# Two token mixers in one kernel: a new written order of all its pieces, and first loads in halves over three queues

## The chip, the cores and the metric

The kernel runs on one NeuronCore of one Trainium2 chip. The metric is the device time of one execution in microseconds (us). Three executions of the kernel before took 786.13, 786.30 and 788.06 us; the median is 786.3.

## What is computed

The reference chains two blocks. The first is a recurrent attention over 768 steps for 4 batches and 8 heads with a state of 40 by 40; the second is a feed-forward block on 3072 tokens of width 320 with a hidden width of 2048 and the activation h cos(h).

```python
for t in range(S):                                  # S = 768
    y[:, :, t] = einsum('bhd,bhde->bhe', r_t, state)
    Sa = einsum('bhde,bhe->bhd', state, a_t)
    state = state * w_t - outer(Sa, b_t) + outer(v_t, k_t)
x = y.transpose(0, 2, 1, 3).reshape(3072, 320)
h = x @ w_in                                        # 320 x 2048
out = (h * cos(h)) @ w_out                          # 2048 x 320
```

The arrays r, k, v, w, a, b are float32; w_in and w_out arrive as 8-byte numbers and are turned into float32 on the chip.

## The kernel before

**Tiling.** The 768 steps are cut into 24 chunks of 32 (C = 32). A chunk has 4 batches times 32 steps = 128 partitions. Within a chunk the recurrence is written as small matrix products with one triangular inverse per chunk; four chunks share one inversion. From chunk to chunk only the state is handed on. Two chunks make one group of the feed-forward block (line 95): 256 tokens, 12 groups. A group walks over the hidden width in 4 parts (j = 0 to 3).

**The order is written out by hand.** All instructions of the kernel are issued by one string, PLAN (lines 17 to 93), of some 1200 tokens. Each token calls one small function (table ACTS, line 954), which emits instructions on several engines. Every engine executes its own instructions strictly in the order in which the tokens stand, so the string fixes five queues at once: TensorE (PE), VectorE (DVE), ScalarE (ACT), GpSimd (POOL) and SyncE (SP, which issues DMAs). A wait at the head of one queue holds everything behind it on that engine.

**Tokens of the attention, for chunk c.** `L` and `ld` load one of r, k, v, w, a, b (line 229): four DMAs, one for each batch, of 40 KB each. `L:c:name:queue:part` of the start names the queue (s = SP, a = ACT, p = POOL) and the part: l = batches 0 and 1, r = batches 2 and 3, x = all four. The tiles of r, k and v exist once (line 216), so the load of the next chunk waits until POOL has read the last one. `pw`, `pa`, `pb`, `pn` (lines 425 to 524) transpose w, a, b of two chunks, scan the decay, form reciprocals (line 452) and the coupling matrix. `sf`, `sc`, `ss` (lines 242 to 263) fetch w of four later chunks, scan it on DVE (nine instructions) and store it. `is`, `ip`, `it`, `ih`, `F`, `S` (lines 531 to 618) invert the triangular matrix of four chunks: `is` transposes, the 15 steps `ip` are DVE alone, `it` and `ih` transpose on DVE, and `F` and `S` complete the off-diagonal halves with 64 tiny matmuls each. `in` and `kn` (lines 620 to 629) are POOL: they copy v and r to padded tiles and multiply k. `v`, `k`, `g` transpose v, r, k and form their products on PE (lines 631 to 686). `t`, `q`, `x`, `s`, `z` (lines 689 to 818) are the chain from chunk to chunk; `z` ends in eight DVE instructions (lines 803 and 810) and five POOL instructions (804 and 815). `tk` stores the chunk's result to DRAM and `tb` loads it back transposed as tokens xT, both by SP (lines 820 to 840).

**Tokens of the weights.** Twenty pieces of w_in and w_out: `wf` fetches (SP), `wt` takes exponent and mantissa apart (two DVE instructions, one ACT), `wm` makes the mantissa (one DVE, one ACT), `wg` sets the sign and `wp` multiplies (one DVE each); lines 300 to 341.

**Tokens of the feed-forward block, for group g and part j.** `fa` and `fb` are the first product (lines 843 to 897) with the phase instructions on ACT and DVE behind them, `y` is the rest of the cosine and the product (lines 887 to 900), `sd` the second product (line 902), `o` the store (line 917). `fa:0:0` can start when tokens of chunks 0 and 1 are back.

**Filling.** `B`, `K` and `P` (lines 924 to 951) emit matmuls on a zero tile, whose results nobody uses.

```python
"L": first_load, "ld": lambda c, n: load(c, n),
...
for token in PLAN.split():
    do(token)
```

Of the kernel before, what the change touches and what calls it, by code (L numbers as in the profile page):

```python
# [38 lines left out]
ss:3 kn:6 ld:7:k r:10 pb:8 fa:1:2 q:5 fb:1:2 pn:8 in:6 sd:1:1:0 y:1:2:1 y:1:2:0 x:5 y:1:2:2 sd:1:1:1 fa:1:3  # L39
ld:7:r s:5 sp:8 ld:7:v S:4:2:1 fb:1:3 y:1:3:0 y:1:3:1 z:5 sd:1:2:1 S:4:3:1 tk:5 t:6 r:11 v:6 k:6 pw:10 pa:10  # L40
ld:12:b g:6 tb:5 ld:12:w y:1:3:2 o:0:1 pb:10 kn:7 sd:1:2:0 pn:10 k:7 in:7 v:7 r:12 fa:2:0 is:8 ij:8:31 ij:8:30
q:6 fb:2:0 y:2:0:1 x:6 sd:1:3:1 y:2:0:0 y:2:0:2 ld:13:a ij:8:29 ij:8:28 ld:8:v ij:8:27 ij:8:26 ld:8:r sd:1:3:0
ij:8:25 ld:12:a s:6 o:1:0 in:8 sd:2:0:0 fa:2:1 ij:8:24 fb:2:1 z:6 ld:8:k kn:8 y:2:1:1 y:2:1:0 sd:2:0:1 y:2:1:2
g:7 fa:2:2 ld:13:w v:8 k:8 pw:12 t:7 ld:9:v ij:8:23 ij:8:22 ij:8:21 ij:8:20 ij:8:19 pa:12 q:7 tk:6 fb:2:2 x:7
ij:8:18 ij:8:17 ij:8:16 ld:13:b sd:2:1:0 tb:6 ld:14:a s:7 y:2:2:0 y:2:2:1 ld:9:k r:13 y:2:2:2 sd:2:1:1 ld:9:r
in:9 z:7 ij:8:15 ij:8:14 fa:2:3 fb:2:3 y:2:3:1 g:8 o:1:1 ld:14:w ij:8:13 ij:8:12 sd:2:2:0 y:2:3:0 sf:4
sd:2:2:1 kn:9 ij:8:11 ij:8:10 k:9 v:9 ij:8:9 y:2:3:2 t:8 tk:7 ij:8:8 g:9 ij:8:7 ij:8:6 sd:2:3:1 ij:8:5 ij:8:4
tb:7 fa:3:0 ij:8:3 ij:8:2 ld:14:b q:8 ld:10:v ld:10:r fb:3:0 ld:15:w in:10 y:3:0:0 ld:15:b ij:8:1 x:8 pb:12
sd:2:3:0 ie:8 y:3:0:2 ld:10:k y:3:0:1 sc:4 s:8 fa:3:1 fb:3:1 y:3:1:1 z:8 ld:15:a o:2:0 sd:3:0:0 tk:8 y:3:1:0
ld:11:r y:3:1:2 sd:3:0:1 sd:3:1:0 pn:12 r:15 sp:12 t:9 fa:3:2 o:2:1 q:9 fb:3:2 x:9 y:3:2:1 sd:3:1:1 y:3:2:0  # L50
y:3:2:2 kn:10 ld:11:k s:9 k:10 pw:14 v:10 fa:3:3 r:14 tb:8 z:9 fb:3:3 y:3:3:0 ld:11:v ld:16:b g:10 sd:3:2:1
y:3:3:1 pb:14 tk:9 t:10 pa:14 kn:11 k:11 in:11 y:3:3:2 ss:4 tb:9 pn:14 sd:3:2:0 ld:16:w r:16 fa:4:0 q:10
fb:4:0 x:10 is:12 ij:12:31 v:11 sd:3:3:1 ij:12:30 ij:12:29 ij:12:28 y:4:0:1 ld:12:v ij:12:27 y:4:0:0 ij:12:26
ij:12:25 ld:16:a ld:12:r y:4:0:2 sd:3:3:0 o:3:0 ij:12:24 ij:12:23 in:12 fa:4:1 sd:4:0:0 ld:17:w s:10 fb:4:1
y:4:1:1 y:4:1:0 ld:12:k z:10 y:4:1:2 tk:10 ld:17:a sd:4:0:1 g:11 t:11 fa:4:2 ij:12:22 ij:12:21 tb:10 ij:12:20
sd:4:1:0 ij:12:19 ij:12:18 ij:12:17 q:11 fb:4:2 x:11 kn:12 k:12 ld:17:b pw:16 ij:12:16 ij:12:15 v:12 ij:12:14
pa:16 ld:18:a s:11 sd:4:1:1 r:17 y:4:2:1 ld:13:v y:4:2:0 y:4:2:2 o:3:1 ld:18:w ij:12:13 z:11 ld:13:k fa:4:3
fb:4:3 ij:12:12 ij:12:11 tk:11 y:4:3:0 g:12 ld:13:r in:13 sd:4:2:0 sd:4:2:1 y:4:3:1 ij:12:10 kn:13 sf:5 v:13
k:13 y:4:3:2 ij:12:9 t:12 ij:12:8 g:13 ij:12:7 ij:12:6 ij:12:5 ij:12:4 ij:12:3 ij:12:2 sd:4:3:0 tb:11 ld:19:b
ij:12:1 ld:14:k ie:12 fa:5:0 ld:18:b q:12 ld:14:r fb:5:0 y:5:0:1 y:5:0:0 x:12 sd:4:3:1 y:5:0:2 sd:5:0:1 sc:5  # L60
ld:19:w fa:5:1 s:12 ld:14:v in:14 fb:5:1 y:5:1:0 z:12 tk:12 o:4:0 sd:5:0:0 pb:16 y:5:1:1 sp:16 t:13 pn:16
o:4:1 ss:5 kn:14 k:14 v:14 pw:18 y:5:1:2 fa:5:2 ld:19:a r:18 r:19 q:13 fb:5:2 y:5:2:1 x:13 sd:5:1:1 s:13
y:5:2:0 y:5:2:2 ld:15:r sd:5:1:0 z:13 ld:20:w tb:12 sd:5:2:0 fa:5:3 g:14 ld:15:k ld:15:v kn:15 ld:20:b fb:5:3
y:5:3:1 sd:5:2:1 pb:18 tk:13 t:14 pa:18 tb:13 y:5:3:0 y:5:3:2 in:15 k:15 r:20 fa:6:0 q:14 fb:6:0 pn:18 y:6:0:1
v:15 is:16 ij:16:31 ij:16:30 ij:16:29 ij:16:28 ld:16:v ij:16:27 ld:21:w sd:5:3:0 y:6:0:0 y:6:0:2 x:14 ij:16:26
ij:16:25 ld:20:a ld:16:r o:5:0 in:16 ij:16:24 sd:5:3:1 ld:17:r fa:6:1 ij:16:23 ld:21:b s:14 fb:6:1 ld:21:a
y:6:1:1 y:6:1:0 z:14 r:21 tk:14 sd:6:0:0 v:16 t:15 ij:16:22 ij:16:21 ij:16:20 g:15 sd:6:0:1 y:6:1:2 fa:6:2
tb:14 q:15 ij:16:19 ij:16:18 ij:16:17 fb:6:2 sd:6:1:0 y:6:2:0 x:15 ld:16:k kn:16 ld:17:k ij:16:16 pw:20 pa:20
k:16 ld:22:a s:15 sd:6:1:1 y:6:2:2 y:6:2:1 z:15 ij:16:15 ij:16:14 ld:22:w ij:16:13 o:5:1 fa:6:3 fb:6:3 y:6:3:1
ld:17:v in:17 g:16 ij:16:12 ij:16:11 ij:16:10 kn:17 sd:6:2:1 sd:6:2:0 y:6:3:0 tk:15 tb:15 y:6:3:2 fa:7:0  # L70
ij:16:9 ij:16:8 t:16 v:17 k:17 ld:22:b q:16 ld:23:w ij:16:7 ld:18:r fb:7:0 g:17 ij:16:6 y:7:0:0 y:7:0:2
ld:18:k sd:6:3:0 y:7:0:1 ld:18:v ij:16:5 in:18 ij:16:4 pb:20 x:16 sd:6:3:1 ij:16:3 ij:16:2 ld:23:b ij:16:1
fa:7:1 ie:16 s:16 sd:7:0:0 ld:23:a fb:7:1 z:16 kn:18 y:7:1:0 o:6:0 y:7:1:1 r:23 o:6:1 sd:7:0:1 tk:16 pn:20
y:7:1:2 r:22 fa:7:2 t:17 sp:20 pw:22 v:18 tb:16 k:18 pa:22 q:17 fb:7:2 y:7:2:1 x:17 sd:7:1:0 ld:19:r s:17
sd:7:1:1 ld:19:k y:7:2:0 y:7:2:2 z:17 ld:19:v kn:19 sd:7:2:1 fa:7:3 fb:7:3 g:18 sd:7:2:0 tk:17 t:18 y:7:3:1
y:7:3:0 y:7:3:2 pb:22 tb:17 k:19 fa:8:0 fb:8:0 y:8:0:1 q:18 y:8:0:0 pn:22 sd:7:3:0 is:20 in:19 ld:20:r
ij:20:31 y:8:0:2 sd:7:3:1 ij:20:30 ij:20:29 x:18 ij:20:28 ld:20:v ij:20:27 ij:20:26 v:19 fa:8:1 s:18 fb:8:1
# [924 lines left out]
```

## Time and profile before

| what | us |
|---|---|
| median of the runs | 786.3 |
| the profiled execution | 787.34 |
| its span, first to last instruction | 785.6 |
| PE busy | 743.9 (95%) |
| DVE busy | 488.4 (62%) |
| ACT busy | 386.2 (49%) |
| POOL busy | 173.4 (22%) |

The profiled execution has 1.7 us outside its span, and is 1.0 us above the median of the runs.

The profile is that of one execution. A row of the timeline gives the start from the span's start, the time, the engine, the line of the kernel, the operation, what it writes and reads, and in square brackets how long the engine sat idle before it and what ended that. "issue" means that nothing in the profile explains the wait. Sums below are made against this execution's own time and then set against the median.

### The profile page before, as it was taken

What the parts mean: (1) busy time and instruction counts of PE and PEld (TensorE: products, weight loads), DVE (VectorE), ACT (ScalarE), POOL (GpSimd) and SP (SyncE); (2) the same over time, 40 slices, a digit from 0 to 9 for tenths busy, and PEclk for the clock granted to TensorE, in tenths of its full rate; (3) what the DMA queues carried; (4) which work ended last, traced back from release to release, by engine and by line L of the source; (5) the groups of instructions that cost most, each with busy time, mean ns of one, the idle gap of its engine ahead of it and who ended that gap; (6) DMA issues with size and microseconds to landing.
All of it is one profiled execution on the core that took longest, in us unless ns stands there. A gap on an engine that the chain in (4) does not pass through costs nothing.

```text
span 785.6 us, 39628 instructions
## 1 busy us (share of the span) xinstructions
PE 743.9 (95%) x17828; PEld 574.8 (73%) x17828; DVE 488.4 (62%) x1095; ACT 386.2 (49%) x772; POOL 173.4 (22%) x334
## 2 busy tenths in 40 slices
PE   5767899998999999999999999999999999999997
...
DVE  7979789884555787545876447776536684333331
...
PEclk9959999998999999999999999999999999999999
...
GB/s 96 157 179 158 146 147 116 107 90 47 103 67 68 50 104 53 55 86 39 46 118 34 99 75 39 50 79 43 48 46 10 58 46 36 37 15 39 19 18 17
DMA packets 183304, 55.79 MB, mean 71 GB/s; under 512 B 157152, under 2 KB 178656, under 8 KB 183136
## 3 DMA queue, kind: packets, MB, share of 16 engines
...
q8 instruction: 140, 2.29, 1.2%
q0 software_dynamic: 256, 0.33, 0.2%
...
q14 instruction: 28, 0.23, 0.1%
...
## 4 chain that ended last, share of the span: by engine, by line
PE 86%; DMA 3%; issue 3%; SPq 2%; POOL 2%; DVE 2%; ACT 1%; ACTq 0%; POOLq 0%; DVEq 0%
PE ph L184 28%; PE po L184 27%; PE x0ps L184 5%; PE dps L184 5%; PE gram L184 4%; PE sps L184 3%; PE vT L408 2%; PE qps L184 2%; SPq L235 2%; PE sT L694 2%; PE below L184 1%; PE wT L408 1%; PE busy L184 1%; PE nps L184 1%; PE kT L408 1%
## 5 line engine op out<-in xcount | busy, mean ns | idle before, releaser
L184 PE MATMUL po<-w_out_sb,gT 128*128 128x320 f32 x768 | 225.6, 440 | 2.8 <-issue 1.5
L184 PE MATMUL ph<-xT,w_in_sb 128*128 128x256 f32 x768 | 185.9, 388 | 1.0 <-issue 0.5
L184 PEld LDWEIGHTS po<-w_out_sb,gT 128*128 128x128 f32 x768 | 140.6, 190 | 59.4 <-issue 5.9
L184 PEld LDWEIGHTS ph<-xT,w_in_sb 128*128 128x128 f32 x768 | 142.1, 191 | 33.6 <-issue 12.4
L884 DVE SCALAR_TENSOR_TENSOR turns<-turns,ph 128x512 f32<-128x512 f32 x96 | 64.2, 684 | 128.2 <-ACT turns L882 128.0
L882 ACT ACTIVATE turns<-ph,rnd 128x512 f32<-128x512 f32 x96 | 64.1, 687 | 118.3 <-PE ph L184 115.3
L804 POOL TENSOR_TENSOR qz<-qz,wc 128x160 f32<-128x160 f32 x92 | 40.5, 465 | 253.6 <-DVE qz L803 253.6
L892 DVE TENSOR_TENSOR gT<-ph,turns 128x512 f32<-128x512 f32 x96 | 65.1, 685 | 40.9 <-ACT turns L889 40.9
L889 ACT ACTIVATE turns<-turns,half_pi 128x512 f32<-128x512 f32 x96 | 69.5, 724 | 3.1
L888 ACT ACTIVATE turns<-turns 128x512 f32<-128x512 f32 x96 | 60.0, 625 | 6.9 <-DVE turns L884 6.8
L184 PE MATMUL ph<-xT,w_in_tail 64*64 64x256 f32 (+1 forms) x528 | 54.2, 392 | 0.0
L712 ACT COPY qz<-qps 40x256 f32<-40x256 f32 x92 | 33.8, 367 | 37.1 <-PE qps L184 35.4
L546 DVE TENSOR_TENSOR inv<-inv,inv_tmp 128x31 f32<-128x31 f32 (+15 forms) x124 | 47.5, 383 | 4.3
L452 DVE RECIPROCAL rw<-nat_w 128x320 f32<-128x320 f32 x20 | 42.8, 2142 | 7.3 <-DMA nat_w<-wd 7.3
L542 DVE TENSOR_TENSOR inv_tmp<-u,inv 128x31 f32<-128x31 f32 (+15 forms) x124 | 44.7, 361 | 3.1
L803 DVE TENSOR_TENSOR qz<-dps,qz 128x160 f32<-128x160 f32 x92 | 29.1, 316 | 17.6 <-PE dps L184 17.4
L756 ACT COPY sm<-sps 128x160 f32<-128x160 f32 x48 | 13.9, 293 | 52.1 <-PE sps L184 42.8
L184 PEld LDWEIGHTS ph<-xT,w_in_tail 64*64 64x64 f32 (+1 forms) x528 | 31.9, 157 | 9.3 <-issue 5.3
L815 POOL TENSOR_TENSOR yt<-yt,wb 128x512 f32<-128x512 f32 x24 | 32.0, 1332 | 23.0 <-DVE yt L810 23.0
L453 POOL TENSOR_TENSOR bn<-nat_b,rw 128x320 f32<-128x320 f32 x22 | 19.3, 879 | 73.7 <-DVE rw L452 26.9
...
L673 ACT COPY vvm<-gram 128x128 f32<-128x128 f32 x48 | 12.2, 264 | 39.0 <-PE gram L184 29.4
...
## 6 DMA issues: line engine op xcount, KB each, us to landing
...
```

The costliest lines, as they stand in the source:

```text
L184: nc.tensor.matmul(o, lhsT=lhsT, rhs=rhs, start=start, stop=stop, skip_group_check=True)
L452: nc.vector.reciprocal(rw, wn)
L542: nc.vector.tensor_tensor(tmp, u[:, j : j + 1, :j].to_broadcast([P, C - j, j]), x[:, j:, j : j + 1].to_broadcast([P, C - j, j]), ALU.mult,)
L546: nc.vector.tensor_tensor(x[:, j:, :j], x[:, j:, :j], tmp, ALU.subtract)
L712: nc.scalar.copy(pick(qz[rows], f * (NZ - C), (NZ, 2 * B), (1, C)), ps[f][rows, : 2 * B * C].rearrange("p (i t) -> p i t", t=C),)
L804: nc.gpsimd.tensor_tensor(z, z, wc.rearrange("p (f m b) -> p f m b", f=2, m=2)[:, :, :, bb] .unsqueeze(3).to_broadcast([P, 2, 2, D]), ALU. ...
L815: nc.gpsimd.tensor_tensor(yt.rearrange("p j b t -> p (j b) t"), yt.rearrange("p j b t -> p (j b) t"), wx, ALU.mult)
L882: nc.scalar.activation(t, u, ACTF.Identity, bias=rnd, scale=1.0)
L884: nc.vector.scalar_tensor_tensor(t, t, -ROUND, u, ALU.add, ALU.subtract)
L888: nc.scalar.activation(t, t, ACTF.Abs)
L889: nc.scalar.activation(t, t, ACTF.Sin, bias=half_pi, scale=-2.0 * math.pi)
L892: nc.vector.tensor_tensor(gT[:, 2 * e : 2 * e + 2, :n], phs[e], ns[e].rearrange("p (f t) -> p f t", f=2), ALU.mult)
```

## The change

Only the string PLAN changes. The same pieces are issued, with the same number of filling matmuls (78 in `B`, 98 in `K`, 60 in `P`) and the same 20 weight pieces, in another order from the first token to the last. Two things are different besides the order. The loads of chunks 0 to 3 (six names, four chunks, four batches: 96 DMAs) are all written in halves of two batches: 48 half loads stand where there were 10 whole loads of a, b and w, 4 halves of w, and 11 `ld` tokens for r, k and v. And 38 of these 96 DMAs are on POOL's queue instead of 8; 4 stay on ACT's, 54 are on SP's. From chunk 4 on, all loads are on SP as before.

The diff, cut to the start, the first inversion of chunks 4 to 7, and the end:

```diff
-L:2:w:s:x L:1:w:a:r L:1:a:s:x B:4 L:0:w:a:r L:0:w:s:l L:1:w:s:l L:3:w:s:x L:0:a:s:x L:0:b:p:x L:3:b:s:x
-L:2:b:s:x L:1:b:p:x pw:0 pa:0 pw:2 pb:0 L:3:a:s:x B:4 L:2:a:s:x pa:2 pn:0 B:4 pb:2 lo:0 sf:1 sc:1 pn:2 lo:2
-ld:0:vr in:0 v:0 sp:0 wf:1 wt:1 ld:0:k B:3 is:0 ip:0:15 ip:0:14 ip:0:13 ip:0:12 B:5 ip:0:11 ip:0:10 kn:0
-ld:1:r wf:0 k:0 ip:0:9 g:0 ip:0:8 ip:0:7 ip:0:6 ip:0:5 ip:0:4 ip:0:3 ld:1:k ld:1:v kn:1 ip:0:2 ip:0:1 it:0
-ih:0 B:4 ss:1 k:1 in:1 v:1 g:1 x:0 ld:2:k F:0:0:0 wm:1 wf:2 wt:2 wm:2 S:0:0:0 wf:3 wg:2 wg:1 ld:2:r wp:1 s:0
-B:3 wp:2 wt:0 wf:4 wf:7 ld:2:v wt:3 wm:0 z:0 sf:2 B:5 t:1 wm:3 F:0:1:0 wg:3 B:6 wf:6 wg:0 wp:0 wp:3 B:3 q:1
-wt:7 wt:4 wm:4 wm:7 wg:4 wp:4 in:2 ld:3:r wg:7 wf:8 kn:2 ld:3:k x:1 wp:7 wf:5 K:6 wf:10 B:5 wf:9 k:2 S:0:1:0
-K:14 wt:6 wm:6 v:2 wt:8 wm:8 wg:6 wp:6 wg:8 g:2 K:4 tk:0 wt:5 wm:5 ld:3:v wg:5 wp:5 wp:8 B:6 s:1 B:4 B:2 wt:10
-wf:11 wt:9 wm:9 B:4 wg:9 z:1 F:0:2:0 B:4 wm:10 wg:10 B:3 in:3 B:3 wp:10 tb:0 wf:12 S:0:2:0 B:6 t:2 tk:1 wp:9
-wf:13 kn:3 K:6 q:2 K:6 wt:12 tb:1 v:3 ld:4:k wm:12 k:3 wg:12 wt:11 wp:12 wg:11 x:2 wm:11 fa:0:0 wt:13 wm:13
-wp:11 ld:4:r wg:13 wp:13 fb:0:0 y:0:0:1 y:0:0:0 wf:14 wt:14 ld:5:a y:0:0:2 wm:14 wf:16 g:3 wf:15 wt:16 wm:16
-ld:4:w K:29 wg:14 wp:14 fa:0:1 F:0:3:1 wf:17 wg:16 fb:0:1 ld:5:w s:2 ld:4:a wt:15 S:0:3:1 wp:16 wt:17 wm:15
-sd:0:0:0 y:0:1:1 y:0:1:0 wg:15 wp:15 sd:0:0:1 z:2 y:0:1:2 ld:4:b wf:19 fa:0:2 pw:4 t:3 ld:4:v in:4 r:4 ld:5:b
-pa:4 wf:18 r:5 q:3 ld:6:w fb:0:2 wt:19 y:0:2:0 x:3 K:13 wg:19 wm:19 sd:0:1:0 y:0:2:2 sd:0:1:1 ld:7:w wm:17
-wg:17 ld:7:b wp:17 y:0:2:1 s:3 pb:4 kn:4 wt:18 wm:18 pw:6 sc:2 K:20 tk:2 pn:4 lo:4 wp:19 fa:0:3 ld:6:b ld:7:a
-r:7 wg:18 r:6 fb:0:3 y:0:3:0 z:3 sd:0:2:0 ld:6:a pa:6 ld:5:k t:4 y:0:3:1 ld:5:v pb:6 v:4 sp:4 y:0:3:2 tb:2
-kn:5 ld:5:r pn:6 is:4 ip:4:15 k:4 lo:6 in:5 k:5 sd:0:2:1 ip:4:14 ip:4:13 ip:4:12 ip:4:11 ip:4:10 ip:4:9 g:4
-ip:4:8 ss:2 v:5 tk:3 tb:3 ld:8:w fa:1:0 ld:9:w ld:8:a ip:4:7 ip:4:6 sf:3 ip:4:5 ld:9:b wp:18 ip:4:4 ip:4:3
-ip:4:2 q:4 ld:6:k ld:9:a ld:6:r fb:1:0 y:1:0:1 ip:4:1 it:4 g:5 ih:4 y:1:0:0 sd:0:3:1 y:1:0:2 r:9 ld:11:b x:4
-sd:0:3:0 F:4:0:1 F:4:1:1 S:4:0:1 fa:1:1 pw:8 pa:8 ld:10:a ld:8:b r:8 ld:10:b ld:10:w fb:1:1 F:4:3:1 s:4
-sd:1:0:0 z:4 y:1:1:1 ld:6:v sd:1:0:1 ld:11:w y:1:1:0 o:0:0 ld:11:a tk:4 F:4:2:1 S:4:1:1 t:5 tb:4 y:1:1:2 sc:3
...
-fa:9:2 tk:20 x:21 sd:9:1:0 s:21 fb:9:2 y:9:2:0 y:9:2:1 ld:23:r tb:20 z:21 y:9:2:2 tk:21 sd:9:1:1 tb:21 fa:9:3
-g:22 t:22 ld:23:v sd:9:2:1 q:22 kn:23 fb:9:3 y:9:3:0 y:9:3:2 sd:9:2:0 y:9:3:1 x:22 in:23 v:23 k:23 fa:10:0
-s:22 fb:10:0 y:10:0:1 y:10:0:0 sd:9:3:0 z:22 sd:9:3:1 tk:22 g:23 y:10:0:2 t:23 fa:10:1 q:23 o:9:0 fb:10:1
-sd:10:0:0 y:10:1:1 y:10:1:0 y:10:1:2 o:9:1 x:23 tb:22 sd:10:0:1 fa:10:2 s:23 fb:10:2 y:10:2:0 sd:10:1:0
-y:10:2:2 z:23 y:10:2:1 tk:23 tb:23 sd:10:1:1 fa:10:3 fb:10:3 y:10:3:1 sd:10:2:1 sd:10:2:0 y:10:3:0 y:10:3:2
-fa:11:0 fb:11:0 y:11:0:1 y:11:0:0 y:11:0:2 sd:10:3:0 o:10:0 sd:10:3:1 fa:11:1 fb:11:1 y:11:1:1 y:11:1:0
-sd:11:0:0 o:10:1 sd:11:0:1 y:11:1:2 fa:11:2 fb:11:2 y:11:2:0 y:11:2:1 y:11:2:2 sd:11:1:1 sd:11:1:0 fa:11:3
-fb:11:3 y:11:3:1 y:11:3:0 y:11:3:2 sd:11:2:1 sd:11:2:0 sd:11:3:0 sd:11:3:1 o:11:0 o:11:1
+L:1:a:p:r L:1:w:a:r L:0:w:s:l L:0:b:s:l B:3 L:0:a:p:r L:0:w:a:r L:1:w:s:l L:3:a:s:l L:2:w:s:r L:3:w:s:r
+L:0:a:p:l L:2:w:s:l L:1:a:s:l L:0:b:s:r L:2:a:p:l L:1:b:p:l L:3:w:s:l L:1:b:s:r L:2:b:p:l pw:0 L:3:b:s:r
+L:3:b:s:l pa:0 L:3:a:p:r pw:2 L:2:b:s:r L:2:a:s:r B:4 pa:2 pb:0 B:2 pn:0 sf:1 sc:1 L:0:v:s:r L:0:r:s:r wf:1
+B:3 sp:0 pb:2 pn:2 L:0:v:s:l lo:2 L:0:r:s:l B:4 lo:0 L:0:k:p:l is:0 wt:1 in:0 ip:0:15 ip:0:14 L:0:k:s:r wf:0
+wm:1 L:1:r:s:l ip:0:13 ip:0:12 ip:0:11 L:1:r:p:r ip:0:10 ip:0:9 kn:0 L:1:k:p:l L:1:k:s:r v:0 k:0 ip:0:8 B:4
+L:1:v:s:l ip:0:7 g:0 ip:0:6 wg:1 B:4 x:0 ip:0:5 ip:0:4 ip:0:3 ip:0:2 ip:0:1 L:1:v:p:r kn:1 in:1 L:2:v:p:r k:1
+v:1 g:1 L:2:v:p:l it:0 wf:2 wt:2 B:5 B:5 wm:2 F:0:0:0 L:2:k:s:r B:4 B:3 ih:0 wg:2 L:2:r:p:l S:0:0:0 wp:2 wp:1
+ss:1 s:0 wt:0 wf:3 wt:3 L:2:r:p:r wg:0 wf:4 wf:5 B:4 wm:0 wg:3 z:0 K:14 t:1 K:4 L:2:k:s:l q:1 wp:0 wm:3 wt:4
+B:3 wm:4 wp:3 F:0:1:0 wg:4 wf:6 wt:6 wm:6 kn:2 k:2 wg:6 wp:6 in:2 B:3 wp:4 wf:7 wt:7 wm:7 x:1 B:4 v:2 S:0:1:0
+wg:7 wf:8 wt:8 wf:9 L:3:v:p:l B:5 s:1 L:3:v:s:r L:3:r:s:l wm:8 tk:0 wp:7 wg:8 wt:9 wm:9 wg:9 wp:8 wp:9 F:0:2:0
+B:6 g:2 B:6 L:3:r:p:r in:3 wf:10 wf:11 wt:10 wm:10 wg:10 sf:2 z:1 wf:12 K:6 wp:10 v:3 t:2 wt:11 wm:11 tk:1 q:2
+wt:5 wm:5 K:6 wg:11 L:3:k:p:r L:3:k:p:l kn:3 tb:0 wp:11 B:6 wt:12 wg:5 S:0:2:0 wm:12 K:6 tb:1 x:2 wp:5 wg:12
+wp:12 k:3 wf:13 wt:13 wg:13 fa:0:0 fb:0:0 wm:13 y:0:0:1 s:2 g:3 ld:4:v y:0:0:0 wf:14 ld:4:k y:0:0:2 wt:14
+wm:14 wp:13 K:29 ld:4:w fa:0:1 wg:14 F:0:3:1 fb:0:1 wp:14 S:0:3:1 y:0:1:0 sd:0:0:1 wf:16 wt:16 wm:16 sd:0:0:0
+wf:15 wt:15 ld:4:a y:0:1:2 ld:5:a y:0:1:1 wg:16 wg:15 z:2 ld:4:b r:4 ld:5:w fa:0:2 t:3 pw:4 wp:16 ld:5:b r:5
+pa:4 wm:15 wf:17 q:3 wt:17 wm:17 sc:2 fb:0:2 ld:4:r sd:0:1:0 x:3 kn:4 wg:17 wp:17 y:0:2:1 pb:4 K:13 y:0:2:0
+ld:7:w wf:19 ld:6:w ld:6:b in:4 tk:2 sd:0:1:1 wf:18 wp:15 wt:19 wm:19 ld:5:r s:3 pw:6 ld:7:b y:0:2:2 ld:5:k
+wg:19 r:7 K:20 r:6 fa:0:3 pn:4 lo:4 fb:0:3 y:0:3:0 wt:18 z:3 sd:0:2:0 pb:6 ld:6:a ld:7:a pa:6 v:4 wm:18 pn:6
+y:0:3:2 wg:18 ld:5:v kn:5 y:0:3:1 sp:4 tb:2 tk:3 k:4 wp:19 in:5 is:4 lo:6 ip:4:15 ip:4:14 ip:4:13 k:5 sd:0:2:1
+ld:8:a g:4 tb:3 ip:4:12 ip:4:11 ip:4:10 fa:1:0 ss:2 ld:8:w ld:8:b wp:18 ip:4:9 ip:4:8 ld:9:w ip:4:7 ld:9:a
+ip:4:6 ip:4:5 ip:4:4 ip:4:3 v:5 t:4 fb:1:0 g:5 q:4 y:1:0:1 ip:4:2 y:1:0:0 sd:0:3:0 o:0:0 ip:4:1 it:4 x:4
+y:1:0:2 sd:0:3:1 F:4:0:1 sf:3 ih:4 ld:6:k pw:8 pa:8 ld:9:b ld:6:r fa:1:1 ld:6:v in:6 r:9 S:4:0:1 fb:1:1
+ld:11:w s:4 F:4:1:1 sd:1:0:0 r:8 ld:10:w ld:10:b ld:10:a o:0:1 z:4 y:1:1:1 sd:1:0:1 S:4:1:1 y:1:1:0 y:1:1:2
+F:4:2:1 kn:6 ld:7:v t:5 ld:7:k ld:11:b pb:8 tk:4 fa:1:2 q:5 fb:1:2 F:4:3:1 x:5 r:10 sd:1:1:0 sp:8 pn:8 r:11
+y:1:2:0 y:1:2:1 ld:11:a y:1:2:2 sc:3 ld:7:r sd:1:1:1 fa:1:3 s:5 fb:1:3 z:5 kn:7 y:1:3:0 tk:5 sd:1:2:1 S:4:2:1
...
+sd:9:1:1 y:9:2:0 y:9:2:1 sd:9:1:0 ld:23:v kn:23 y:9:2:2 g:22 sd:9:2:0 fa:9:3 t:22 in:23 v:23 k:23 q:22 tb:21
+fb:9:3 y:9:3:0 y:9:3:1 x:22 y:9:3:2 sd:9:2:1 fa:10:0 s:22 fb:10:0 y:10:0:1 y:10:0:0 y:10:0:2 sd:9:3:0 o:9:0
+sd:9:3:1 z:22 tk:22 fa:10:1 t:23 g:23 q:23 sd:10:0:0 tb:22 x:23 fb:10:1 y:10:1:1 y:10:1:0 sd:10:0:1 y:10:1:2
+s:23 fa:10:2 fb:10:2 y:10:2:0 y:10:2:1 z:23 sd:10:1:1 sd:10:1:0 o:9:1 y:10:2:2 fa:10:3 fb:10:3 y:10:3:0 tk:23
+sd:10:2:0 sd:10:2:1 y:10:3:1 y:10:3:2 tb:23 fa:11:0 fb:11:0 y:11:0:1 y:11:0:0 y:11:0:2 sd:10:3:1 sd:10:3:0
+fa:11:1 fb:11:1 y:11:1:1 y:11:1:0 y:11:1:2 o:10:0 o:10:1 sd:11:0:1 sd:11:0:0 fa:11:2 fb:11:2 y:11:2:0 y:11:2:1
+sd:11:1:0 y:11:2:2 sd:11:1:1 fa:11:3 fb:11:3 y:11:3:1 sd:11:2:0 sd:11:2:1 y:11:3:0 y:11:3:2 sd:11:3:0 o:11:0
+sd:11:3:1 o:11:1
```

More of the change, by code (lines that the diff above doesn't have):

```diff
@@ L38 @@
-sd:1:0:0 z:4 y:1:1:1 ld:6:v sd:1:0:1 ld:11:w y:1:1:0 o:0:0 ld:11:a tk:4 F:4:2:1 S:4:1:1 t:5 tb:4 y:1:1:2 sc:3
[L39 to L77, printed above, removed]
@@ L78 @@
-y:8:1:1 y:8:1:0 z:18 sd:8:0:1 g:19 y:8:1:2 ld:20:k kn:20 sd:8:0:0 ij:20:25 ij:20:24 tk:18 tb:18 fa:8:2 P:60
-t:19 k:20 ij:20:23 ij:20:22 ij:20:21 ij:20:20 o:7:0 in:20 v:20 q:19 ij:20:19 fb:8:2 y:8:2:0 y:8:2:1 x:19
-ld:21:v ld:21:r in:21 sd:8:1:0 ij:20:18 ij:20:17 ij:20:16 g:20 s:19 sd:8:1:1 y:8:2:2 ld:21:k z:19 fa:8:3
-sd:8:2:1 ij:20:15 ij:20:14 o:7:1 ij:20:13 ij:20:12 ij:20:11 ij:20:10 ij:20:9 t:20 v:21 kn:21 k:21 q:20 fb:8:3
-y:8:3:1 y:8:3:0 y:8:3:2 x:20 ij:20:8 ij:20:7 ij:20:6 ij:20:5 ij:20:4 ij:20:3 ij:20:2 ld:22:k ij:20:1 ie:20
@@ L83 @@
-sd:8:2:0 tk:19 tb:19 fa:9:0 ld:22:r fb:9:0 y:9:0:1 y:9:0:0 sd:8:3:1 y:9:0:2 sd:8:3:0 g:21 s:20 fa:9:1 ld:22:v
-in:22 sd:9:0:0 z:20 o:8:0 fb:9:1 y:9:1:1 kn:22 ld:23:k o:8:1 sd:9:0:1 k:22 t:21 v:22 y:9:1:0 y:9:1:2 q:21
-fa:9:2 tk:20 x:21 sd:9:1:0 s:21 fb:9:2 y:9:2:0 y:9:2:1 ld:23:r tb:20 z:21 y:9:2:2 tk:21 sd:9:1:1 tb:21 fa:9:3
-g:22 t:22 ld:23:v sd:9:2:1 q:22 kn:23 fb:9:3 y:9:3:0 y:9:3:2 sd:9:2:0 y:9:3:1 x:22 in:23 v:23 k:23 fa:10:0
-s:22 fb:10:0 y:10:0:1 y:10:0:0 sd:9:3:0 z:22 sd:9:3:1 tk:22 g:23 y:10:0:2 t:23 fa:10:1 q:23 o:9:0 fb:10:1
```

45 lines of the change are left out of this document (added).

## The prediction

> **What bounds the kernel now.** I read the 40 slices first. Each is 19.6 us; the digits are tenths of busy time.
>
> ```profile
> PE   5767899998999999999999999999999999999997
> DVE  7979789884555787545876447776536684333331
> PEclk9959999998999999999999999999999999999999
> ```
>
> From the fifth slice on, PE is full to the end. Before that it is not, while DVE is. The busy times by stretch, which I asked for next, make this exact (the second column is the length, then PE, PEld and DVE).
>
> ```profile
> 0.00:100.00 100.00, 72.82 (x2118) 51.40 (x2119) 82.62 (x174) 40.11 (x83) 34.04 (x76) 0.88 0.62 146
> 100.00:160.00 60.00, 58.99 (x1489) 48.20 (x1489) 53.35 (x108) 39.68 (x75) 16.57 (x33) 1.00 0.53 119
> 160.00:200.00 40.00, 36.27 (x1070) 28.29 (x1059) 24.26 (x58) 15.27 (x35) 6.70 (x13) 0.91 0.39 72
> 200.00:786.00 586.00, 575.80 (x13178) 446.91 (x13176) 328.20 (x758) 291.14 (x580) 116.12 (x212) 1.00 0.26 53
> ```
>
> PE idles 27.2 us in the first 100, 1.0 in the next 60, 3.7 in the next 40, and 10.2 in the last 586, of which 5.5 is the tail after the last matmul (780.1). PE's real work is the same in both orders. So the time is: when the feed-forward work starts (fa:0:0, at 99.15), plus PE's work from there, plus what PE loses later. Before 99, DVE's queue and the chain of chunks decide; these rows of DVE's timeline show where DVE itself waits.
>
> ```profile
> 48.68 0.68 DVE L331 SCALAR_TENSOR_TENSOR mant<-words,mant 128x512 f32<-128x512 uint32 x1
> 52.46 0.29 DVE L615 TENSOR_TENSOR rt<-rt,below 128x128 f32<-128x128 f32 x1 [3.10 <-PE below L184]
> 59.30 0.33 DVE L803 TENSOR_TENSOR qz<-dps,qz 128x160 f32<-128x160 f32 x1 [1.44 <-PE dps L184]
> 96.91 0.69 DVE L325 SCALAR_TENSOR_TENSOR expo<-words,expo 128x512 int32<-128x512 int32 x1 [2.86 <-ACT expo L322]
> ```
>
> **A, the first loads.** Now SP issues w of chunk 2 and a of chunk 1 ahead of the two halves of w that `pw:0` needs, and PE starts late:
>
> ```profile
> 9.05 1.09 PE L408 MATMUL wT<-ident,nat_w 128*128 128x128 f32 x4 [1.82 <-DMA nat_w<-in_w_dram]
> ```
>
> In the new order these halves are SP's issues 1, 2, 5 and 6. SP issues one per 0.49 us (7.27, 7.77, 8.28 in its timeline), so the sixth stands at 3.3 to 4.4, and with 1.8 from that issue to landing (7.27 to 9.05) w is there by 6.2. PE's filling `B:3` ends at 5.34 + 3 x 0.47 = 6.75: gain 2.3. Then a of chunk 0 decides, now on POOL as its issues 3 to 6. What POOL's DMAs cost is shown by the eight of b:
>
> ```profile
> L235 POOL DMA_DIRECT2D nat_b<-in_b_dram x8: 584/584/752, 5.2 to 9.4; - x8
> DMA to landing us min/median/max: 3.2/3.6/3.8
> ```
>
> The sixth starts at 5.23 + 0.75 + 4 x 0.58 = 8.3 and lands at 11.9, and the transposes of a then run 1.9 earlier than now (13.94). POOL's twelve issues end at 12.4, its three small ones (0.21, 0.21, 0.13) at 13.0, and only then may DVE's aT go (now 15.14). I take a gain of 1.7; ends 0 (POOL's issues slower beside DVE's scans) and 2.3.
>
> **B, the inversion.** The 3.10 comes from PE: its timeline has F:0:0:0 cut by an "issue" gap of 3.58 at 46.77, and the 1.44 before z:0 contains another of 1.16. The new order puts wt:2, wm:2 (0.84 + 0.68) and ih:0 (1.90) on DVE between it:0 and the wait, so F and such a gap lie beside DVE's work. What is late next is chunk 1: g:1 now stands before it:0 in DVE's queue. From the reciprocals 1.7 earlier and wt:1 moved behind is:0 (0.75), is:0 starts at 31.55 - 2.45 = 29.1; to it:0 it was 11.7, plus wt:1, wm:1, wg:1, x:0 (0.75, 0.68, 0.69, 0.45): DVE is at g:1 at 43.4. POOL, after sp:0 (29.65 - 1.8 = 27.8 now minus the copies in:0 that stood before it, 1.7: 26.1), has L:0:k (2 x 0.58), in:0 (1.7), L:1:r (1.2), kn:0 (1.4), L:1:k and L:1:v (2.3): 33.9, landing 3.6 after the last issue 37.0, kn:1 and in:1 2.3, then PE v:1 1.0, two ACT copies 1.1, g:1 1.3 to 2.6: 42.7 to 44. So some 0.5 of wait there, 0.5 at S:0:0:0 and 0.5 at s:0, which now follows S by only 1.4 of DVE work. Gain 4.5 - 1.5 = 3.0; I take 2.5; ends -1.5 (one gap of 3.6 falls on the path again, and POOL is late) and 4.5.
>
> **C, from z:1 to fa:0:0.** Summed in queue order with each instruction's mean, DVE has 70.0 us of work before z:1 now and 69.2 then: 0.8. From DVE's first instruction of z:1 (85.60) to fa:0:0 (99.15) it is 13.55, because F:0:2, ten fillings, S:0:2 and six more stand on PE before t:2, and ACT then holds wg:12 back (the 2.86). In the new order t:2 follows z:1 at once. Late next is k:3: POOL is through z:1 after 3.8 (89.42), four DMAs for k 2.3, landing 3.0 more, kn:3 0.9, its transpose 0.4 and the rest of the way 0.7: 11.1. The tokens' way (xd out 89.45, xT out to 93.3, landing about 2) is 9.7. Gain 2.4; ends 0 and 3.5.
>
> So fa:0:0 moves from 99.15 to 99.15 - 1.7 - 2.5 - 0.8 - 2.4 = 91.8.
>
> **D, group 1.** Between fa:0:0 and fa:1:0 the work is the same, except that t:4 and v:5 go behind fa:1:0, and the store of the scanned decay (`ss:2`), which now runs beside the tokens' transfer (the chain has "154.00 5.04 DMA xd<-yt", against 2.3 for chunk 1), goes behind it. PE's tokens g:4, v:5 and fa:1:0 take 2.5 more there than elsewhere. Gain 1.5; ends 0 and 2.5.
>
> **E, the burst at 176.**
>
> ```profile
> 175.74 1.28 PE L184 MATMUL below<-rn,noff 32*32 32x16 f32 x128
> 179.96 0.83 PE L184 MATMUL below<-rt,half 32*32 32x16 f32 x47 [2.75 <-issue]
> 180.72 3.78 PE L184 MATMUL ph<-xT,w_in_sb 128*128 128x256 f32 x8
> 184.29 1.91 PE L408 MATMUL wT<-ident,nat_w 128*128 128x128 f32 x8
> ```
>
> F, F, S back to back are 192 tiny matmuls, and PE waits 2.75 for nothing the profile shows; after it fa:1:1 takes 3.57 to the next token (1.82 elsewhere), pw:8 1.71 (0.87), pa:8 1.16 (0.88): 2.9 at half clock. The page's queue line "q8 instruction: 140, 2.29, 1.2%" says what comes in there: 140 packets of 16 KB; PE's 35,656 matmuls and weight loads make about 256 to a packet, and no two packets start closer than 3.4 apart. 256 of these tiny instructions run in 1.2 to 1.6 us. The Trainium skill says the same of the size (Runtime: NRT & Kernel Launch, Terms: an engine's instruction memory is refilled in 16 KiB blocks); the trace agrees, with 140 packets of 16384 bytes. The new order puts pw:8, pa:8 and fa:1:1 between F and S, and the other F and S apart too. Gain 5.6 at best, 0 if the gap only moves; I take 4.5.
>
> **F, after 200.** PE's order is new everywhere. The pairs that matter keep their cover, with few exceptions: t:23 follows z:22 by one fa (1.82) where 3.0 was the least cover without a wait now: 1.2; q:20 follows t:20 by 0.5 of PE work against ACT's two copies of 1.0: 0.5. That is -1.7. For waits that no view of before can show I set 3.0, two thirds of the 4.7 that PE idles there now; ends 0 and 6. The tail is unchanged: both orders end in two second products, a copy and a store.
>
> **Sum.** 1.7 + 2.5 + 0.8 + 2.4 + 1.5 + 4.5 - 1.7 - 3.0 = 8.7. The profiled execution took 787.3 (span 785.6): 778.6. The median is 1.0 below that execution: **777.6**.
>
> **Rivals.** *Slower through POOL.* Eight of POOL's issues lie between sp:0 and kn:1, and four before kn:3, all on the path above, beside a busy DVE; the trace has POOL's DMAs only beside an idle one (0.58) and beside one memset (0.75). For it: POOL's other work does stretch (kn from 0.86 to 1.30 at 64.8), and DVE's too (wg from 0.69 to 1.75). Against it: most of the DMA's time needs no operand. If an issue waits out one DVE instruction (0.69) it costs 1.3: 12 x 0.7 = 8 us, and the gain is gone; this is the deciding point. If it waits out the longest (the 2.14 of a reciprocal), 2.7: 12 x 2.1 = 25, 803. At 2.0 between them, 17 us: 795. The Trainium skill (SBUF — State Buffer, A bandwidth-pool intuition that's wrong) has a DMA from GpSimd at 620 ns alone and 3100 ns beside a copy of DVE, and says under Who interferes with whom that tensor_tensor does not stall it so; the 0.58 agrees with the first figure and no run here shows the second. By the second alone, an estimate from that page, twelve would cost 30 us.
>
> *It does not do what it says.* DVE's queue is the bound up to is:4: 135.3 us of work in both orders, from 10.44 to 156.2. If its waits only change place, A is all that is left: 785.6 or, with F's losses, about 786.
>
> *Slower through bursts.* Each new place where tiny matmuls bunch costs what E shows, 5.6. Two of them and no gain in E: 778.6 + 4.5 + 5.6 x 1.3, about 790.
>
> **Numbers.** Forecast 0.64, its own range 769 to 785; POOL 0.17 at 795; nothing 0.12 at 786; bursts 0.07 at 790. A measurement of this kernel can tell about 0.3%, 2.4 us, from no change: faster than that 0.65, within it 0.12, slower 0.23. The range goes from 768 (nearly all upper ends) to 793, and leaves out a part of the POOL case.
>
> **What would show it.** A: pw:0 near 6.8. B: no DVE wait above 1 us before S:0:0:0, and g:1 near 43. C: fa:0:0 near 91.8, with kn:3 just before. E: no "issue" gap above 1 us between 165 and 190, and clock 1.0 there. POOL: DMA_DIRECT2D rows of 0.6 beside a busy DVE. The prediction is wrong if these rows are above 1.3, if fa:0:0 stands later than 97, or if PE idles over 10 us between 200 and its last matmul.

## The result and the profile after

Five runs of the changed kernel took 777.06 to 782.45 us, median 778.51; five of the kernel before 786.13 to 788.35, median 786.98. The ratio is **0.9897, 95% interval 0.9867 to 0.9926**: 8.1 us faster (5.8 to 10.5), against a forecast of 777.6. The profiled run was the slowest of its five (782.45, span 780.6), so this profile shows 5.0 of the 8.1; a second profile, of the same kernel run again (after2 below), has a span of 776.7.

The slices and the stretches of the changed kernel, in the columns shown for before:

```profile
PE   5687899989999999999999999999999999999997
DVE  8888889876555886635876746786345883343331
PEclk9889899999999999999999999999999999999999
...
0.00:100.00 100.00, 73.61 (x2122) 53.78 (x2123) 84.07 (x176) 40.10 (x84) 49.09 (x106) 0.90 0.62 141
100.00:160.00 60.00, 57.50 (x1421) 46.39 (x1421) 51.32 (x100) 37.95 (x73) 17.72 (x33) 1.00 0.56 118
160.00:200.00 40.00, 37.02 (x1061) 29.68 (x1059) 25.77 (x63) 17.20 (x38) 7.79 (x16) 0.96 0.46 95
```

The start is hardly denser than before, the next 60 us are less dense (57.5 against 59.0 busy), and the clock between 160 and 200 is 0.96 instead of 0.91. The rest of the gain lies where the slices cannot show it, behind 200. PE's waits from 200 to 780 do. Before:

```profile
PE po L184 <- issue: 1.5, 1, 1.5
PE po L184 <- DVE inv_tmp L542: 1.3, 1, 1.3
PE bT L408 <- issue: 0.7, 1, 0.7
PE kT L408 <- POOL kn L628: 0.3, 1, 0.3
```

and after, the same view, one line:

```profile
PE bT L411 <- DVE vvm L679: 0.2, 1, 0.2
```

To compare orders piece by piece I took for each PE piece the time from its first matmul to that of the next piece, and from it the fastest tenth among the pieces of its kind in all 14 profiles. What is over is called its loss here. The kernels that the columns name are described in the next section. The remaining sum is 695.6 to 695.7 in every kernel, so the losses (us, one profile each) are where kernels differ.

| stretch | before | after | after2 | a_head | b_head | b_spread | b_fetch | a_bunch | a_a3 | b_best |
|---|---|---|---|---|---|---|---|---|---|---|
| to fa:0:0 | 39.9 | 39.2 | 38.9 | 37.0 | 39.2 | 40.1 | 39.0 | 33.9 | 33.4 | 37.2 |
| fa:0:0 to fa:1:0 | 3.9 | 7.6 | 6.5 | 6.0 | 6.2 | 3.9 | 2.8 | 5.5 | 5.9 | 3.2 |
| fa:1:0 to fa:1:2 | 8.3 | 4.4 | 3.0 | 7.0 | 2.5 | 5.0 | 4.0 | 9.8 | 5.4 | 3.1 |
| fa:1:2 to the end | 24.9 | 20.7 | 19.4 | 24.8 | 19.4 | 27.0 | 21.6 | 19.7 | 19.3 | 20.2 |

The gain of the changed kernel is in the last two rows; its first two together are no better than before (46.8 and 45.4 against 43.8).

### The profile page after: what moved, and what is told of

It reads as the page before. It is cut to its first block, busy times and chain, and to the rows that moved or that the text cites. A ratio compares the mean times of both kernels' runs of the same rounds, so it can differ in the third digit from the quotient of the medians.

```text
span 780.6 us, 39597 instructions
## 1 busy us (share of the span) xinstructions
PE 742.6 (95%) x17812; PEld 577.4 (74%) x17812; DVE 489.7 (63%) x1095; ACT 384.0 (49%) x772; POOL 188.8 (24%) x364
## 4 chain that ended last, share of the span: by engine, by line
PE 89%; DVE 3%; DMA 2%; issue 2%; POOL 1%; ACT 1%; SPq 1%; DVEq 0%; ACTq 0%; POOLq 0%
PE ph L187 28%; PE po L187 27%; PE dps L187 5%; PE x0ps L187 5%; PE gram L187 4%; PE vT L411 3%; PE sps L187 2%; PE sT L697 2%; PE qps L187 2%; PE nps L187 2%; PE busy L187 2%; PE below L187 1%; PE kT L411 1%; PE bT L411 1%; PE aps L411 1%
## 5 line engine op out<-in xcount | busy, mean ns | idle before, releaser
L807 POOL TENSOR_TENSOR qz<-qz,wc 128x160 f32<-128x160 f32 x92 | 40.1, 460 | 210.5 <-DVE qz L806 210.5
L456 POOL TENSOR_TENSOR bn<-nat_b,rw 128x320 f32<-128x320 f32 x22 | 19.7, 899 | 110.6 <-DVE rw L455 46.7
L806 DVE TENSOR_TENSOR qz<-dps,qz 128x160 f32<-128x160 f32 x92 | 29.1, 317 | 21.5 <-PE dps L187 21.3
L625 POOL COPY vp<-nat_v 128x320 f32<-128x320 f32 x24 | 11.8, 491 | 93.5 <-DMA nat_v<-in_v_dram 71.1
```

The lines of the kernel that those rows point to most:

```text
L807: nc.gpsimd.tensor_tensor(z, z, wc.rearrange("p (f m b) -> p f m b", f=2, m=2)[:, :, :, bb] .unsqueeze(3).to_broadcast([P, 2, 2, D]), ALU. ...
```

## The experiments

Each ratio below is to runs of the kernel before that were timed beside it, and kernels timed at different times are compared by these ratios. Runs of one kernel spread over 3 to 10 us, so a profile is one draw, and differences of a few us between two profiles are not by themselves a result. Theory: the gain is the packing of the tiny matmuls behind fa:0:0, which PE's instruction fetch cannot follow when they bunch. Rival (the prediction's own sum): most of it is the quicker start.

**Cut at fa:0:0.** a_head is the new start with the old rest, b_head the old start with the new rest.

```diff
 a_head: tokens of the new PLAN ahead of fa:0:0, then
-fa:0:0 wt:13 wm:13 wp:11 ld:4:r wg:13 wp:13 fb:0:0
+fa:0:0 ld:4:k wm:13 ld:4:r wp:13 fb:0:0
 ...
 b_head: tokens of the old PLAN ahead of fa:0:0, then
-fa:0:0 fb:0:0 wm:13 y:0:0:1 s:2 g:3 ld:4:v y:0:0:0 wf:14 ld:4:k
+fa:0:0 wt:13 wp:11 wg:13 fb:0:0 wm:13 y:0:0:1 s:2 g:3 ld:4:v y:0:0:0 wf:14
```

> The new order up to fa:0:0, the old order behind it (the three weight pieces that the new start has done already are left out of the rest, one load of chunk 4 is put into it). The prediction's sum put 7.4 of the gain ahead of fa:0:0: by it 787 - 7.4 = 779.6. The profile of the new kernel has fa:0:0 only 0.75 earlier, with about 2 us more of DVE's work done by then: by it 785 to 786.5. The first is my forecast, the second the reading of the trace; I hold the second.

> The old order up to fa:0:0, the new one behind it: the other half of the same cut. If the gain lies ahead of fa:0:0, as the prediction had it, 785 to 787. If it lies behind it (the reading of the trace), 779 to 781.

a_head: 0.9997 (0.9972 to 1.0022). b_head: 0.9881 (0.9854 to 0.9909). All of the gain that these runs can show is behind fa:0:0, and the rival falls; a_head's interval leaves room for 2.2 us at most. In a_head's profile fa:0:0 stands at 96.24, 2.9 earlier than in that of before, but fa:1:0 only 0.8 earlier (161.08): the lead is gone again before group 1.

**The burst at 176.** b_spread is the old order with the two F and the S apart; a_bunch is the new order with them together again.

```diff
 b_spread
-F:4:0:1 F:4:1:1 S:4:0:1 fa:1:1 pw:8 pa:8
+F:4:0:1 pw:8 pa:8 F:4:1:1 fa:1:1 S:4:0:1
 a_bunch
-F:4:0:1 sf:3 ih:4 ld:6:k pw:8 pa:8 ld:9:b ld:6:r fa:1:1 ld:6:v in:6 r:9 S:4:0:1 fb:1:1 ld:11:w s:4 F:4:1:1
+F:4:0:1 sf:3 ih:4 F:4:1:1 S:4:0:1 ld:6:k fa:1:1 pw:8 pa:8 ld:9:b ld:6:r ld:6:v in:6 r:9 fb:1:1 ld:11:w s:4
```

> The old order with one edit: pw:8, pa:8 and fa:1:1 are put between the first F, the second F and the S that stood back to back at 176. If the three in a row outrun PE's instruction fetch, and the half clock behind them follows from it, the gap of 2.75 and the 2.9 of half clock go: 781.5 to 782.5 against 787. If the gap only moves to the next tiny matmuls, or DVE or ACT hold PE there instead: 786 to 787.

> The new order with one edit: the second F and the S of the second inversion stand directly behind the first F again, ahead of pw:8, pa:8 and fa:1:1, as they did before. If it is three in a row that cost 5.8 us there, 4.5 to 6 above the changed kernel and a gap of more than 2 us near 180, which ends 2.0 to 2.7 us after the start of an instruction packet. If it was the moment of the packet in the old order and not the bunch: no change, within 1 us.

> The changed kernel once more, as the measure for the others of this call and for a second profile: 778 to 780 where before is 787, that is a ratio of 0.988 to 0.993. PE's idle time between 200 and its last matmul is below 1 us again (0.2 in its first profile) if the new order takes the gaps away for good; 3 or more if the first profile was lucky.

after2: 0.9903 (0.9870 to 0.9936), and PE's idle time between 200 and its last matmul sums to 0.3 (0.5 in the first profile, 4.3 before). a_bunch: 0.9965 (0.9939 to 0.9990), 0.0062 above after2, which is 4.9 us. PE's timeline of the changed kernel and then of a_bunch, at the same pieces:

```profile
179.52 0.73 PE L187 MATMUL below<-rn,noff 32*32 32x16 f32 x64
180.23 1.06 PE L411 MATMUL wT<-ident,nat_w 128*128 128x128 f32 x8
181.13 1.04 PE L411 MATMUL aps<-ident,nat_a 128*128 128x128 f32 x8
182.00 1.89 PE L187 MATMUL ph<-xT,w_in_sb 128*128 128x256 f32 x8
183.82 0.69 PE L187 MATMUL below<-rt,half 32*32 32x16 f32 x61
184.82 0.23 PE L187 MATMUL below<-rt,half 32*32 32x16 f32 x3 [0.30 <-issue]
```

```profile
172.00 1.29 PE L185 MATMUL below<-rn,noff 32*32 32x16 f32 x128
173.15 0.38 PE L185 MATMUL below<-rt,half 32*32 32x16 f32 x24
177.38 0.73 PE L185 MATMUL below<-rt,half 32*32 32x16 f32 x40 [3.85 <-issue]
178.04 3.78 PE L185 MATMUL ph<-xT,w_in_sb 128*128 128x256 f32 x8
```

With big matmuls between F and S, PE waits 0.30; without, 3.85, and the fa:1:1 behind it takes 3.78 instead of 1.89, at a granted clock of 0.50. The clock is the third number from the end of these rows, first of the changed kernel, then of a_bunch:

```profile
180.20:184.00 3.80, 3.80 (x49) 3.32 (x48) 2.25 (x4) 1.34 (x3) 0.66 (x4) 1.00 0.86 237
178.00:182.50 4.50, 4.50 (x21) 3.64 (x15) 0.29 (x1) 0.00 (x0) 0.00 (x0) 0.50 0.36 59
```

So step E is shown in the new order, gap and half clock. The Trainium skill (TensorE: Matmul & The Clock Gate, Why this matters for your kernels) warns of idle gaps above some 3 us between bursts; here gaps of 2.75 (before) and 3.85 (a_bunch) went with half clock. The length of one gap does not decide it in these traces: a wait of 1.53 in b_spread, which ended at 408.44, had half clock behind it from 408.48 to 411.89, and one of 2.67 in b_head, which ended at 161.95, had none.

b_spread: 0.9981 (0.9956 to 1.0006), less than expected and not to be told from the kernel before. In its profile the stretch loses 5.0 instead of 8.3: a wait of 0.91 in the first F and 1.59 for a load of a are what remains there. And the two larger gaps behind 200 are still there.

**All three large gaps.** b_fetch is the old order with F and S placed as in the new one, and two exchanges behind 200.

```diff
-F:4:0:1 F:4:1:1 S:4:0:1 fa:1:1 pw:8 pa:8 ld:10:a ld:8:b r:8 ld:10:b ld:10:w fb:1:1 F:4:3:1 s:4 sd:1:0:0
+F:4:0:1 pw:8 pa:8 fa:1:1 S:4:0:1 ld:10:a ld:8:b r:8 ld:10:b ld:10:w fb:1:1 s:4 F:4:1:1 sd:1:0:0
 ...
-sd:1:0:1 ld:11:w y:1:1:0 o:0:0 ld:11:a tk:4 F:4:2:1 S:4:1:1 t:5
+sd:1:0:1 S:4:1:1 ld:11:w y:1:1:0 o:0:0 ld:11:a tk:4 F:4:2:1 t:5
 ...
-fb:1:2 pn:8
+fb:1:2 F:4:3:1 pn:8
 ...
-pn:14 sd:3:2:0
+sd:3:2:0 pn:14
 ...
-t:12 ij:12:8 g:13 ij:12:7 ij:12:6 ij:12:5 ij:12:4 ij:12:3 ij:12:2 sd:4:3:0
+t:12 ij:12:8 ij:12:7 ij:12:6 ij:12:5 ij:12:4 ij:12:3 ij:12:2 sd:4:3:0 g:13
```

> The old order with three edits: the pieces F and S of the second inversion stand as in the new order; pn:14 and sd:3:2:0 change places; g:13 goes behind sd:4:3:0. They undo the three gaps behind 165 that end 2.0 to 2.7 after the start of an instruction packet (2.9, 1.9, 1.4 us in the old order; the half clock behind the first is 2.9 more). If these are the gain behind fa:0:0, it is 5 to 8 us faster than before. If the gaps only wander to other bunches, as two did in the run of the spread F and S, 0 to 3.

b_fetch: 0.9945 (0.9918 to 0.9971), 4.3 us faster than before (2.3 to 6.4), between its two expectations. Its waits from 200 to 780 are down to two:

```profile
PE nps L183 <- issue: 0.5, 1, 0.5
PE bT L407 <- issue: 0.2, 1, 0.2
```

Six moved pieces, none of them a load, give about half of what the 1200 tokens give. What names the cause is the packets in which PE's instructions come in, by a DMA queue of their own (q8 on the page): in the old order such packets start at 177.59, 348.03 and 408.08, and the three gaps end at 179.96, 350.31 and 410.62, 2.3 to 2.5 later. Over all 14 profiles, 82 of the 90 PE gaps above 0.5 us that the profile calls "issue" end 1.9 to 2.75 after a packet's start, and the other eight 2.8 to 3.1 after one. Packets start 4.5 to 4.8 apart in the median, so by chance fewer than one gap in five would end in a stretch of 0.85. The gap at 410, which the profile puts down to DVE's inv_tmp, ends in the same way, though the DVE instruction that feeds sd:4:3:0, the gT product, ended at 406.5. In profiles b_fetch loses no more than b_head (67.4 and 67.3 in sum), but timed it is 0.6% slower. b_fetch's profile is of one of its faster runs (777.90, where its twelve go from 776.76 to 782.76), b_head's of the slowest of six (777.70), so what b_fetch's slower runs lose stands in no profile. What the other half comes from is open.

**The start's own terms.** In a_a3 one half load goes ahead of pw:0 on POOL; in a_sp all 38 POOL loads are issued by SP at the same places (every `p` of an `L` becomes `s`).

```diff
 a_a3
-L:2:b:p:l pw:0 L:3:b:s:r L:3:b:s:l pa:0 L:3:a:p:r pw:2
+L:2:b:p:l L:3:a:p:r pw:0 L:3:b:s:r L:3:b:s:l pa:0 pw:2
 a_sp
-L:1:a:p:r
+L:1:a:s:r
...
```

> The new order with one edit: the half load of a for chunk 3 on GpSimd's queue goes ahead of pw:0. In the changed kernel it stands behind POOL's work of pa:0, is issued at 17.17, and pa:2 waits 2.8 for it. Alone: pa:2 does not wait, is:0 and fa:0:0 come about 2 earlier. If an earlier start is handed through to the end: 2 below the changed kernel, a ratio of 0.987 to 0.988 (it had 0.990). If the stretch up to fa:1:0 is held by SP's loads and the tokens of chunk 3 whatever the start does: the same as it, 0.989 to 0.992, with fa:0:0 earlier and fa:1:0 where it was.

> The new order, but the 38 loads on GpSimd's queue are issued by SP, at the same places of the order. If the second queue is what makes the start quicker, the loads of k, r and v come late by up to 38 x 0.49 = 18 us of SP's issues, much of it hidden: 782 to 787. If the start is held by DVE's queue and by what PE lacks there, 777 to 780. If POOL's issues cost (0.58 each, 30 more than before), it is faster: 774 to 777.

a_sp: 0.9962 (0.9942 to 0.9982), 0.0059 above after2. PE waits 4.95 for the a of chunk 3 and the first inversion starts at 35.68 instead of 31.0 to 31.9: within the new start the second queue is worth its place. POOL's price is in the changed kernel's own rows:

```profile
17.17 1.18 POOL L238 DMA_DIRECT2D w_in_sb<-in_a_dram  x2
18.34 0.21 POOL L444 COPY wc<-wb 128x16 f32<-128x16 f32 x1
...
37.17 2.33 POOL L238 DMA_DIRECT2D nat_v<-in_v_dram  x4
39.49 2.30 POOL L238 DMA_DIRECT2D nat_r<-in_r_dram  x4
```

0.58 each, at 37 to 42 beside a DVE that runs one TENSOR_TENSOR after the other; the longest of all 38 is 0.75. The rival by POOL's price is excluded. The 3100 ns of the Trainium skill (SBUF — State Buffer, A bandwidth-pool intuition that's wrong) appear in no row of this start. Its DVE runs no COPY beside these DMAs: 34 of the 38 lie beside TENSOR_TENSOR, scans, reciprocals, transposes, memsets, SCALAR_TENSOR_TENSOR or, eight times, a TENSOR_SCALAR.

a_a3: 0.9889 (0.9869 to 0.9909), not to be told from after2 by time. Its profile shows what the prediction overlooked. PE's timeline at the transposes of a (aps) of chunk 3, first in the changed kernel, then in a_a3:

```profile
19.56 0.66 PE L478 MATMUL wn<-ident,wb 128*128 128x128 f32 x4 [0.18 <-DVE wb L438]
23.02 0.63 PE L411 MATMUL aps<-ident,w_in_sb 128*128 128x128 f32 x4 [2.81 <-DMA w_in_sb<-in_a_dram]
```

```profile
19.94 0.65 PE L476 MATMUL wn<-ident,wb 128*128 128x128 f32 x4 [0.18 <-DVE wb L436]
20.43 0.60 PE L409 MATMUL aps<-ident,w_in_sb 128*128 128x128 f32 x4
```

The load stands behind pa:0 in the order, so on POOL behind the two products bn of pa:0, which wait for DVE's reciprocals; it is issued at 17.17. Without that, is:0 starts on DVE at 30.06 (three profiles with the edit: 30.05, 30.06, 30.06) instead of 31.0 to 31.9 (five profiles of the new start without it). In a_a3's profile fa:0:0 stands at 92.67 and fa:1:0 at 155.87 (163.26 and 161.93 in the two of the changed kernel). That the edit does this is not shown, since a_bunch, without it, has 93.16 and 155.87, and the runs give back nothing that can be told from zero.

**Ahead of fa:1:0.** b_best (old start, new rest), a_best (the changed kernel) and a_both (that with a_a3's edit) have two edits on SP's queue; a_z is a_both with one tiny piece moved.

```diff
 b_best, a_best, a_both, a_z
-in:4 tk:2 sd:0:1:1
+in:4 tk:2 ld:6:a ld:7:a sd:0:1:1
 ...
-pb:6 ld:6:a ld:7:a pa:6
+pb:6 pa:6
 ...
-ld:8:a g:4 tb:3
+g:4 tb:3 ld:8:a
 a_z, besides
-wp:9 F:0:2:0 B:6 g:2
+wp:9 B:6 g:2
 ...
-v:3 t:2 wt:11
+v:3 t:2 F:0:2:0 wt:11
```

> The old start, the new order behind fa:0:0, and there two edits on SP's queue: the loads of a for chunks 6 and 7 stand 25 places earlier, and the load of a for chunk 8 goes behind tb:3. Theory: fa:1:0 waits for the tokens of chunk 3, and the second inversion for these loads of a; both come earlier, and the time is 1.5 to 4 below that of the old start with the new order behind it (776.9 where before was 784.8): a ratio of 0.983 to 0.987. Rival: DVE's queue holds the stretch, and nothing changes (0.988).

> The new order with the two edits on SP's queue ahead of fa:1:0 (the loads of a for chunks 6 and 7 earlier, that of chunk 8 behind tb:3), its own start kept. These edits moved fa:1:0 from 162 to 157 in the profile behind the old start. The same here: PE does not wait before fa:1:0, which stands 3 to 5 earlier, and the time is 2 to 4 below the changed kernel: 0.986 to 0.988. If the runs give nothing back for it (as 0.993 in the runs behind the old start lets me fear): 0.990 to 0.993, and fa:1:0 earlier all the same.

> Both: the half load of a for chunk 3 early, and the two edits on SP's queue. If the start's gain was only lost because the stretch to fa:1:0 was held by SP, both together give more than their sum: fa:1:0 at 153 to 156 and 4 to 7 below the changed kernel, 0.982 to 0.985. If PE's work and DVE's queue are the bound there, no more than the better of the two: 0.987 to 0.991.

> The run with both, and F:0:2:0 behind t:2 instead of ahead of g:2, so that 64 tiny matmuls fewer stand in the 18 us before z:1 (593 of them and of fillings now, which is 4.6 packets of 256 instructions at 3.4 us or more each). If it is the bunch that makes the gap of 2 to 2.9 at 76 to 84, it is gone or below 1, z:1's DVE instructions do not wait, and 1 to 2 are gained on the run with both. If the gap moves behind z:1 or to fa:0:0: no difference.

b_best 0.9927 (0.9896 to 0.9958), a_best 0.9903 (0.9880 to 0.9925), a_both 0.9899 (0.9879 to 0.9920), a_z 0.9920 (0.9902 to 0.9938): none is faster than the changed kernel. The mechanism is there all the same. SP's queue in the changed kernel, with PE's row of fa:1:0:

```profile
155.56 2.40 SPq L828 DMA_DIRECT2D xd<-yt  x2
158.06 1.79 SPq L238 DMA_DIRECT2D nat_a<-in_a_dram  x4
160.00 0.39 SPq L839 DMA_DIRECT2D xT<-xd  x1
160.43 1.92 SPq L841 DMA_DIRECT2D xT<-xd  x2
```

```profile
163.26 1.19 PE L187 MATMUL ph<-xT,w_in_sb 128*128 128x256 f32 x4 [2.36 <-DMA xT<-xd]
```

Four loads of a stand between the store of chunk 3's tokens and their way back, and PE waits 2.36 at the end of that way. In b_best's profile PE does not wait there and fa:1:0 starts at 156.92 (b_head 161.95); in those of a_best, a_both and a_z at 158.0, 155.9 and 158.5. Why the timed runs give nothing back for it is not settled; a_bunch, whose order up to there is that of the changed kernel, had 155.87 in its profile, so one profile cannot carry it. a_z failed outright: z:1 waits 1.90 for DVE and then 3.83 for "issue", and fa:0:0 stands at 98.19.

## Why the prediction was right, and where it was not

The time was right to 0.9 us, the sum behind it was not: the start was to give 7.4 and gave nothing that the runs can show, and the time behind 200 was to cost 4.7 and gave about as much. In the losses of the two profiles F is 9 to 10 us better than forecast, the start 6 to 7 worse and D 4 to 5 worse. That these errors cancel is luck. (The rivals' times, 795, 786 and 790, were set on the profiled execution and so stand 1.0 too high beside the forecast.)

**A failed by a load it did not look at.** pw:0 came at 6.58 (6.8 forecast) and pa:0 2.5 earlier than before. But "the transposes of a then run 1.9 earlier" was worked out for chunk 0 alone; that of chunk 3 waits 2.81, and is:0, after a wait of 2.13 on DVE, stands at 31.89 instead of 29.1. a_a3 takes the wait away: is:0 at 30.06, still 1.0 behind the forecast. fa:0:0 then stands at 92.67, 94.78 (a_both) and, with one more piece moved, 98.19 (a_z), where 91.8 was forecast: an early is:0 alone does not bring it there. Five profiles of the unedited new start have it at 93.2 to 98.4, mean 96.3; five of the old start at 96.5 to 99.4, mean 98.3. So fa:0:0 came 2.0 earlier on average, less than either group spreads, and not 7.4.

**B and C were right in what they looked at.** The first two of these waits are near the forecast ones:

```profile
52.52 0.29 DVE L618 TENSOR_TENSOR rt<-rt,below 128x128 f32<-128x128 f32 x1 [0.32 <-PE below L187]
...
58.60 0.33 DVE L806 TENSOR_TENSOR qz<-dps,qz 128x160 f32<-128x160 f32 x1 [0.84 <-PE dps L187]
...
87.86 0.33 DVE L806 TENSOR_TENSOR qz<-dps,qz 128x160 f32<-128x160 f32 x1 [2.76 <-PE dps L187]
```

3.10 became 0.32 and 1.44 became 0.84, and from the last row's 87.86 to fa:0:0 it is 10.5 (11.1 forecast, 13.55 before). But g:1 was at 46.58 (43.4), A's delay; and the 2.76 is new. F, B:6, g:2, B:6 and z:1 now stand together, and PE has an "issue" gap of 2.63 in z:1: the rival of the bursts in small, at a place that the sum passed over. That F is what makes the bunch too long there is not shown: a_z moves it away, and the gap is 3.83.

**D had the wrong sign.** From fa:0:0 to fa:1:0 it is 64.9 instead of 62.8, and the loss 3.7 higher (2.6 in the second profile), where 1.5 of gain was forecast. The step took the store `ss:2` out of the tokens' way and did not look at the other SP issues there, the loads of a. That these are all of it is not shown.

**E was right.** The losses there fall by 3.9 and 5.3 in the two profiles (4.5 taken), and undoing it in a_bunch costs 4.9 of time. Its sign holds in the first profile for the gap (0.30) and not quite in the second, which has an "issue" gap of 1.02 at 182.53.

**F had the wrong sign.** Its 4.7 of idle behind 200 was taken as a level that any order would have. The largest parts of it were two more of the gaps of E, at 350 and 410; the new order has none. The two named small waits may be there (q's pieces take 1.6 more in the whole of the first profile, 0.6 in the second), but the losses behind fa:1:2 fall by 4.2 and 5.5.

By its own criteria, "fa:0:0 stands later than 97" came true (98.40) and should have made it wrong. The start, as the sum had it, was wrong; the time came out all the same because F's error outweighed it.
